# First head pair of the attention stage: keys and queries turned into two PSUM tiles, its four loads on SP's queue, the first batch's global keys and queries on ACT's queue

## Chip, cores and metric

The kernel runs on one core of a Trainium2 chip. The metric is the device time of one execution in microseconds (us), as the median of several runs. Engines are named as the profile names them: PE is TensorE, DVE VectorE, ACT ScalarE, POOL GpSimd and SP SyncE. SP and ACT both issue DMAs; "SPq" and "ACTq" are rows in which one of them does so.

## What is computed

An attention over local and global tokens (4 batches, 8 heads, 512 local and 32 global tokens, heads of 64), and behind it two gated feed-forward layers over the 2176 tokens that come out, of width 512.

```python
def _attn_ref(q_l, k_l, v_l, q_g, k_g, v_g):
    k_all = np.concatenate([k_g, k_l], axis=2)
    v_all = np.concatenate([v_g, v_l], axis=2)
    out_g = np.matmul(sm(scale * np.matmul(q_g, k_all.transpose(0, 1, 3, 2))), v_all)
    s_ll = np.where(mask, scale * np.matmul(q_l, k_l.transpose(0, 1, 3, 2)), -1e9)   # |i - j| <= 32
    s_lg = scale * np.matmul(q_l, k_g.transpose(0, 1, 3, 2))
    out_l = np.matmul(sm(np.concatenate([s_lg, s_ll], axis=-1)), np.concatenate([v_g, v_l], axis=2))
    return np.concatenate([out_g, out_l], axis=2)
...
x = attention, tokens by 512
x = (silu(x @ w_gate) * (x @ w_val)) @ w_out
h = x @ w_in
out = (h * tanh(softplus(h))) @ w_out2
```

## The kernel before, in words

Everything is in float32. The attention goes by pairs of heads: 16 pairs, four in each batch. Its work is cut into named tasks (line 231), each on one engine, and a string written by hand (`ORDER`, lines 222 to 229, read by `in_order`, line 243) says in which order the tasks are emitted. Each letter stands for a kind of task, and the kind says the engine ("Ak+1" is the keys' copy on its second engine). Nothing is reordered behind that list, so each engine meets its instructions in the order of the list, DMA issues of SP and ACT among them. The feed-forward layers follow under a scheduler of their own (`run`, line 1302), which goes by costs written in the kernel and knows nothing of the attention's times. So the change leaves its order as it was. The weights of the first layer are loaded and converted between the attention's tasks.

The tasks of the first pairs that matter here, with n the pair, b the batch and g the half of a pair's tokens:

- qk(n), `load_qk`, lines 167 to 176: four DMAs of 128 KB, two for the keys (`ks`) and two for the queries (`qs`). All are issued by SP, but for the two of the queries of pair 0, which ACT issues.
- gk(b, 0) and gk(b, 1), `load_glob`, lines 160 to 165: two DMAs of 32 KB each for the global keys of a batch, then two for its global queries, all on SP, into the one buffer `gkq`.
- A(n), line 273, PE: 8 transposes of the keys and 8 of the queries (line 213) into one PSUM tile of two banks. There are two such tiles. Ak(n) (lines 282, 236 and 238) copies the turned keys to `kt`, Aq(n) the turned queries to `qT`. For pair 0, Ak is on ACT and Aq on DVE, and Aq comes after Ak.
- AG(b, 0), line 467, PE: the transpose of the global keys; AGk(b), on ACT for batch 0, copies them to `gkT`. AG(b, 1) is the transpose of the global queries, and AGe(b) on DVE (line 478) scales them into `qgbd`.
- S(n, g), lines 297 to 308, PE: the scores, which need Aq(n), Ak(n) and AGk(b). M(n, g, i) on DVE (line 318) adds the mask and takes the smallest, E(n, g, i) on ACT (line 325) is the exponential.

The list begins: qk(0), A(0), Ak(0), Aq(0), gk(0, 0), AG(0, 0), AGk(0), S(0, 0), three M, E(0, 0, 0), M, qk(1), gk(0, 1), vg(0), qk(2), A(1), AG(0, 1), qk(3), Ak(1), AGe(0), S(0, 1), Aq(1), M, S(1, 0), GA(0), and so on. PE thus has, in this order: A(0), AG(0, 0), S(0, 0), A(1), AG(0, 1), S(0, 1), S(1, 0), GA(0).

Behind some PE tasks stand matmuls of zeros whose result nobody uses (`keep_busy`, line 150): 14 instructions at the start, and so many behind each PE task as the string `steady` (line 539) says: 6 instructions behind AG(0, 0), 2 behind AG(0, 1).

Of the kernel before, what the change touches and what calls it, by code (L numbers as in the profile page):

```python
# [21 lines left out]
def tile_attn_moe_moe2(  # L22
# [15 lines left out]
    nc = tc.nc  # L38
    B, H, SL, D = q_l.shape
# [5 lines left out]
    S = SG + SL  # L45
# [50 lines left out]
    vg = e_p.tile([128, 4, HP, D], F32, name="vg")  # L96
    vgb = e_p.tile([128, H, D], F32, name="vgb")
# [41 lines left out]
    def both(task):  # L139
        return PAIR[place[task]]  # L140
# [4 lines left out]
    QS, KS, VW, GK = {}, {}, {}, {}  # L145
# [4 lines left out]
    def keep_busy(bank, k):  # L150
        for i in range(k):
            nc.tensor.matmul(ONE[bank][:, 0:128], lhsT=zeros, rhs=zeros, start=True, stop=True)
# [7 lines left out]
    def load_glob(b, i):  # L160
        if i == 0:
            GK[b] = g_p.tile([128, 2, 128], F32, tag="gkq", name="gkq")
        for h in range(2):
            nc.sync.dma_start(out=GK[b][:, i, 64 * h:64 * h + 64],
                              in_=(k_g, q_g)[i][b].rearrange("(g h) p d -> h g p d", h=2)[h])

    def load_qk(b, hp):
        hs = slice(2 * hp, 2 * hp + 2)
        qs = qk_p.tile([128, 4, 2, D], F32, tag="qs", name="qs")
        ks = qk_p.tile([128, 4, 2, D], F32, tag="ks", name="ks")  # L170
        eng = nc.sync if b or hp else nc.scalar
        for h in range(2):
            nc.sync.dma_start(out=ks[:, :, h], in_=k_l[b, 2 * hp + h].rearrange("(c p) d -> p c d", p=128))
        for h in range(2):
            eng.dma_start(out=qs[:, :, h], in_=q_l[b, 2 * hp + h].rearrange("(c p) d -> p c d", p=128))
        QS[b, hp], KS[b, hp] = qs, ks

    def load_vg(b):
# [29 lines left out]
    def half(j):  # L208
        return slice(64 * j, 64 * j + 64)

    def transpose_half(out, src, j):

        nc.tensor.transpose(out, src, ident[half(j), half(j)])  # L213
# [2 lines left out]

    tasks = {}
    LETTERS = ascii_letters + digits + "!#$%&()*+-./:;<=>?@[]^_{|}~"
    KINDS = ("qk A Ak+1 Aq+1 gk AG AGk+1 S M E vg AGe Aq GA GG v R GGe w N GM C V+1 vgb GE GR GN D Cq Ak "
             "GT AGk Cf GV V GO Ch Xh Cl Xl Xh+1 GGe+1 GXh GXl F_g Ch+1 Cl+1 Ft F_v Fg Fp GXh+1 Fh Fl "  # L220
             "Fh+1 F2 Fy+1 Fy N+1").split()
    ORDER = "abcdefghiiijiaekabfaclhmihniiiijojphjjjjjiiiqbirjjsettucmveiiiwvwphxjjyzhjjjjABiijqiiiiiibjjjCjfttDEfFmv"
    ORDER += "nGHGvIGjhuIhiiiiJyjjjGqaabpKitBclidtLjjjiipMvvwsjINhzhjijjjiijAajBqtiiiiitLEHNOovPbNIJcCdvnjIheaGGGhiiiB"
    ORDER += "isjQjjjjqRiiibkQLtSppciumtbNyxvGSfwTUjcmjjjvCjjjVzhaAwWiiiihEsGeWiqRBaiXiiYGjjHjjjjGttvvnIGIjjuqythhJpKi"
    ORDER += "iiZiBsjjjpMiiii0btCRvaDSmLgvfSGGGGTIIjjjlhMzhiiiiij1jjjWqttAVbiWXiajLDBjjjmiNYN2vjjvInoqttIOhPE1iBjHuCii"
    ORDER += "jivkOvJGjINhGpSjIyspijiiixNbbjcGWacSjmdzGQjAqVhtthWiiiijeeijjjjERXBYHiiiCvvGaInGGGIhujjjhBiLqityKJiiijLt"
    ORDER += "bNiiiScMmNfvvFKISMzwZfbRjjjAhappaDjmj3ijjjiiiEl4hqstoniBHriiutivvww3yjLjj5jjjjhhiBiiziNiiiJiqjkLbbttjjjj"
    ORDER += "D3pANjjDZmd35jvqv2IntR1Ih4hpxtBiiiiijjVjEWHuXiiijjjjvvWjwwhyqYthiiijj0Jt1BpiiiZiziLjNApjvvjjjj33Rw5w34EL"
    ORDER += "Hq6B65vvw3IBLL5NNJNQRs"

    def task(name, engine, needs, work, banks=0, until=None):
        tasks[name] = engine, [x for x in needs if x is not None], work, banks, until
# [10 lines left out]
    def in_order():  # L243

        left, done = {}, []
        for n in tasks:
            left.setdefault(f"F_{n[3]}" if n[0] == "F" else n[0], []).append(n)
        free = {2: list(range(len(PAIR))), 1: list(range(len(ONE)))}
        until = {}
        for letter in ORDER:  # L250
            kind, _, other = KINDS[LETTERS.index(letter)].partition("+")
            n = left[kind].pop(0)
            engines, needs, _, banks, last = tasks[n]
            ON[n] = engines.split()[int(other or 0)]
            if not all(x in place for x in needs):
                raise RuntimeError(f"{n} comes before what it needs")
            place[n] = free[banks].pop(0) if banks else None
            if banks:
                until[last] = banks, place[n]
            if n in until:  # L260
                free[until[n][0]].append(until[n][1])
            SPARE_BANK[n] = free[1][0] if free[1] else None
            done.append(n)
        return done

    def add_pair(n):
        b, hp = divmod(n, HP)
        ago = lambda name, k: (name, n - k) if n >= k else None
        agog = lambda name, k, g: (name, n - k, g) if n >= k else None
        lastu = lambda name, m: (name, m // 2) if m >= 0 else None  # L270
        R = {}

        def qk():
            p = both(("A", n))
            for i, src in enumerate((KS[b, hp], QS[b, hp])):
                for r in range(4):
                    for j in range(2):
                        transpose_half(p[:, j, 256 * i + 64 * r:256 * i + 64 * r + 64],
                                       src[half(j), r].rearrange("p h d -> p (h d)"), j)
            R["pk"], R["pq"] = (p[:, :, 256 * i:256 * i + 256].rearrange("c j (r t) -> c r j t", t=64) for i in range(2))  # L280

        def keys():
            duplicate(("Ak", n), KT[n % 2][:, SG:SG + SL].rearrange("c (r j t) -> c r j t", j=2, t=64), R["pk"])
# [1 line left out]
        def queries():  # L285
            R["qT"] = qk_p.tile([128, 4, 128], F32, tag="qT", name="qT")
            dst = R["qT"].rearrange("c r (j t) -> c r j t", j=2)
            duplicate(("Aq", n), dst, R["pq"])

        task(("A", n), "PE", [("qk", n)], qk, 2, ("Aq", n))  # L290
        task(("Ak", n), "DVE ACT", [("A", n), lastu("GA", n - 2), agog("S", 2, 1)], keys)
        task(("Aq", n), "ACT DVE",
             [("A", n), ("Ak", n), agog("S", 2, 1)], queries)

# [85 lines left out]
        task(("Xl", n), "DVE", [("Xh", n)], lambda: x_parts(*args(), "l", ("Xl", n)))  # L382

        task(("qk", n), "SP", [ago("A", 2)], lambda: load_qk(b, hp))
        task(("v", n), "SP", [ago("D", 2), lastu("GO", n - 2)], lambda: load_v(b, hp))
        if hp % 2:
# [74 lines left out]
    def add_batch(b):  # L461
# [36 lines left out]
        for i in range(2):  # L498
            task(("gk", b, i), "SP", prev(("AG", b - 1, 1)), lambda i=i: load_glob(b, i))
# [3 lines left out]
    def add_convert(i):  # L503

        gen = None

        def go():
            nonlocal gen
            gen = gen or w_convert(converts.pop(0))
            next(gen, 0)  # L510

        task(("Cq", i), "ACT", [("w", i)] + ([("Cf", i - 1, 0)] if i else []), go)
        for j, room in enumerate((0.70, 1.20, 0.75, 0.80)):
            need = [("Cf", i, j - 1)] if j else [("Cq", i)] + ([("Cf", i - 1, 3), ("Cl", i - 2)][:i] if i else [])
            task(("Cf", i, j), "DVE", need, go)
        task(("Ch", i), "ACT DVE", [("Cf", i, 3)], go)
        task(("Cl", i), "POOL DVE", [("Ch", i)], go)
# [8 lines left out]
    def attention():  # L526


        for b in range(B):
            add_batch(b)  # L530
        for n in range(B * HP):
            add_pair(n)
        for i in range(8):
            task(("w", i), "SP", [("Cf", i - 2, 3)] if i > 1 else [], load_next)
        for i in range(6):
            add_convert(i)
        for i in FILL:
            add_fill(i)
        steady = iter("03001000014100000001")
        for name in in_order():  # L540
            tasks[name][2]()
            if tasks[name][0] == "PE" and SPARE_BANK[name] is not None:
                keep_busy(SPARE_BANK[name], int(next(steady, 0)))
# [165 lines left out]
    with tc.manual_schedule():  # L709
        setup()  # L710
        attention()
# [28 lines left out]
    def slots(p, shape, dtype, names):  # L740
        return [lambda name=name: p().tile(shape, dtype, tag=name, name=name) for name in names]
# [20 lines left out]
    GR = Ring(slots(lambda: s_p, [128, 512], F32, [f"s{i}" for i in range(5)]))  # L762
# [52 lines left out]
    for i in range(6):  # L815
        p = order[i]
# [603 lines left out]
```

## Time and profile before

| | |
|---|---|
| median of 3 runs | 880.22 us (879.88 to 880.99) |
| profiled execution, device time | 879.67 us |
| its span, first to last instruction | 877.9 us |
| mean granted TensorE clock | 0.999 |
| PE busy | 869.5 us, 99% of the span |
| DVE, POOL, ACT busy | 657.3, 519.0, 475.1 us |
| HBM traffic over the span | 176 GB/s |

The rows read for the prediction are all from the one profiled execution, and their times count from the start of its span. A row of the timeline has the start, the duration (of several instructions merged, where it ends with x2 or more, from the start of the first to the end of the last), the engine, the line of the kernel, the operation, the tile that is written and what is read; in brackets, how long the engine had been idle before and what released it.

### The profile page before, as it was taken

To read this page: it belongs to the slowest core of one execution; us is meant where nothing else is said; L and a number is where in the kernel's file an instruction comes from. 1 tells how busy PE (TensorE), PEld (TensorE's weight loads), DVE (VectorE), ACT (ScalarE), POOL (GpSimd) and SP (SyncE) were. 2 spreads that over 40 slices of the span, in tenths; PEclk is the share of its full clock that TensorE was granted. 3 is DMA by queue.
4 is the path that set the end of the run, shared out by engine and by line. 5 is a ranking of instruction groups with operands and counts; after the bars stand their busy time and mean duration, and the time that the engine had idled before them with its cause. 6 is when DMAs were issued, how large, how long until landed. Compare 5 with 4: busy or idle time off the path is not lost.

```text
span 877.9 us, 18526 instructions
## 1 busy us (share of the span) xinstructions
PE 869.5 (99%) x7004; PEld 805.9 (92%) x7004; DVE 657.3 (75%) x1243; ACT 475.1 (54%) x1153; POOL 519.0 (59%) x503
## 2 busy tenths in 40 slices
PE   8999999999999999999999999999999999999998
PEld 7788889989999999999999999898989898989896
DVE  5877777998988878778888899678886767543434
ACT  6888774544345554555555678754545454434341
POOL 4455645999985565566675799455466444433231
PEclk9999999999999999999999999999999999999999
DMA  7986743435556556557546436574747473535173
GB/s 177 207 188 135 169 98 74 161 104 195 182 178 244 174 180 224 173 156 246 174 157 226 157 140 255 171 251 156 264 143 253 164 256 116 184 108 193 58 255 143
DMA packets 157401, 155.61 MB, mean 177 GB/s; under 512 B 78976, under 2 KB 137856, under 8 KB 157312
## 3 DMA queue, kind: packets, MB, share of 16 engines
q1 hardware_dynamic: 155824, 153.38, 55.9%
q8 instruction: 55, 0.90, 0.4%
q10 hardware_dynamic: 1488, 1.05, 0.4%
q14 instruction: 34, 0.28, 0.1%
HBM read 132.12 MB, written 22.28 MB: 176 GB/s over the span
## 4 chain that ended last, share of the span: by engine, by line
PE 98%; DMA 1%; DVE 0%; ACT 0%; issue 0%; SPq 0%
PE p L1106 38%; PE p L1211 21%; PE p L997 15%; PE p L1063 9%; PE one L639 4%; PE pair L213 3%; PE pair L304 2%; PE one L371 2%; PE one L375 2%; PE one L445 1%; PE one L399 1%; PE pair L307 1%; DMA gkq<-in_q_g 1%; DMA ks<-in_k_l 0%; ACT kt L236 0%
## 5 line engine op out<-in xcount | busy, mean ns | idle before, releaser
L1106 PE MATMUL p<-xh,w 128*128 128x384 f32 (+1 forms) x992 | 257.4, 326 | 0.0
L1211 PE MATMUL p<-w,a 128*128 128x512 f32 x816 | 194.3, 391 | 0.0
L1211 PEld LDWEIGHTS p<-w,a 128*128 128x128 f32 x816 | 152.2, 188 | 29.9
L1106 PEld LDWEIGHTS p<-xh,w 128*128 128x128 f32 x992 | 176.8, 188 | 1.4
L1106 PE MATMUL p<-xl,w 128*128 128x384 f32 (+1 forms) x496 | 161.5, 326 | 0.0
L1118 ACT ACTIVATE b<-p 128x384 f32<-128x384 f32 (+1 forms) x144 | 68.1, 473 | 160.6 <-PE p L1106 156.5
L997 PE MATMUL p<-a,w 128*128 128x384 f32 (+2 forms) x768 | 142.8, 334 | 0.0
L997 PEld LDWEIGHTS p<-a,w 128*128 128x128 f32 x768 | 130.6, 188 | 2.8
L1221 DVE TENSOR_TENSOR y<-p,y 128x512 f32<-128x512 f32 x119 | 82.1, 690 | 66.1 <-PE p L1211 64.8
L1027 POOL TENSOR_TENSOR a<-b,a 128x384 fp32r<-128x384 f32 (+1 forms) x57 | 60.4, 1060 | 110.3 <-ACT a L1025 76.7
L810 DVE TENSOR_TENSOR b<-p,b 128x384 f32<-128x384 f32 (+1 forms) x144 | 76.6, 532 | 63.3 <-PE p L1106 48.1
L857 POOL TENSOR_TENSOR w<-cx,w 128x256 fp32r<-128x256 f32 (+1 forms) x94 | 101.5, 1092 | 35.4 <-ACT w L856 30.0
L1106 PE MATMUL p<-e,w 128*128 128x384 f32 (+1 forms) x528 | 100.8, 328 | 0.0
L1027 POOL TENSOR_TENSOR a<-s,a 128x384 fp32r<-128x384 f32 (+2 forms) x54 | 63.9, 1185 | 55.7 <-ACT a L1025 55.5
L1106 PEld LDWEIGHTS p<-xl,w 128*128 128x128 f32 x496 | 93.1, 188 | 1.4
L1106 PEld LDWEIGHTS p<-e,w 128*128 128x128 f32 x528 | 90.0, 188 | 1.1
L1006 DVE TENSOR_TENSOR y<-p,y 128x384 f32<-128x384 f32 (+2 forms) x116 | 62.7, 543 | 19.7 <-PE p L997 18.5
L1063 PE MATMUL p<-xh,w 128*128 128x384 f32 (+1 forms) x256 | 72.7, 356 | 0.0
L580 DVE SCALAR_TENSOR_TENSOR fl<-q,st 128x512 f32<-128x512 f32 x68 | 62.0, 912 | 5.0 <-ACT q L572 4.8
L1025 ACT ACTIVATE a<-s 128x384 fp32r<-128x384 f32 (+2 forms) x88 | 45.2, 515 | 37.7 <-DVE s L1049 36.7
L584 DVE SCALAR_TENSOR_TENSOR cx<-fl,cx 128x512 uint32<-128x512 uint32 x68 | 63.5, 934 | 1.1
L586 DVE SCALAR_TENSOR_TENSOR cx<-st,cx 128x512 uint32<-128x512 uint32 x68 | 63.3, 932 | 0.7
(151 smaller groups left out, 1486.6 us busy)
## 6 DMA issues: line engine op xcount, KB each, us to landing
e<-td SPq DMA_DIRECT2D x76, 384.0 KB, 4.2
xh<-td SPq DMA_DIRECT2D x38, 384.0 KB, 3.3
xl<-td SPq DMA_DIRECT2D x38, 384.0 KB, 4.1
st<-in_moe_w_out SPq DMA_DIRECT2D x28, 512.0 KB, 3.7
st<-in_moe_w_in SPq DMA_DIRECT2D x16, 512.0 KB, 4.1
vw<-in_v_l SPq DMA_DIRECT2D x14, 512.0 KB, 6.2
e<-td SPq DMA_DIRECT2D x22, 320.0 KB, 5.6
st<-in_moe_w_gate SPq DMA_DIRECT2D x12, 512.0 KB, 4.7
```

The source lines that it names most:

```text
L584: nc.vector.scalar_tensor_tensor(x, fu, 0xC0000000, x, op0=ALU.bitwise_and, op1=ALU.bitwise_or)
L586: nc.vector.scalar_tensor_tensor(x, STG.pop(p)[:, :, 0], 29, x, op0=ALU.logical_shift_right, op1=ALU.bitwise_or)
L810: return lambda e: vec(e).tensor_tensor(out=out(), in0=a(), in1=b(), op=op)
L857: add(lo or [("POOL", PO(n))], 0, lambda e: vec(e).tensor_tensor(out=dst(1), in0=src(), in1=dst(0).bitcast(F32), op=ALU.subtract), r=[rd, ...
L997: nc.tensor.matmul(ps.h[:, 0:n], lhsT=a.h[:, d], rhs=b.h[:, at:at + n], start=(i == 0 and j == 0), stop=(i == len(ws) - 1 and j == 2))
L1006: add("DVE", DV(n), lambda e: nc.vector.tensor_tensor(out=ya, in0=ps.h[:, 0:n], in1=ya, op=ALU.add), r=[ps], w=yt)
L1027: t.append(add(either(n), 0, lambda e: vec(e).tensor_tensor(out=dst(1), in0=get(), in1=dst(0).bitcast(F32), op=ALU.subtract), r=[v, (av[0] ...
L1063: nc.tensor.matmul(ps.h[:, 0:n], lhsT=a.h[:, d], rhs=b[:, c, c0:c0 + n], start=(c == 0 and j == 0), stop=(c == KD - 1 and j == 2))
L1106: nc.tensor.matmul(ps.h[:, 0:n], lhsT=w.h[:, 256 * a + 128 * c:256 * a + 128 * c + 128], rhs=xs[b][:, c, :], start=(start and c == 0 and j ...
L1118: add("ACT", AC(n), lambda e: nc.scalar.activation(out=dst.h[:, 0:n], in_=src.h[:, 0:n], func=AF.Copy), r=[sv], w=[dst])
L1211: nc.tensor.matmul(ps.h, lhsT=a.h[:, d], rhs=b.h, start=(i == 0 and q == 0), stop=(i == len(ws) - 1 and q == 2))
L1221: add("DVE", DV(512), lambda e: nc.vector.tensor_tensor(out=ya, in0=pa(), in1=ya, op=ALU.add), r=[ps], w=tok)
```

## The change

The two DMAs of pair 0's queries go to SP's queue, behind those of its keys. The four DMAs of batch 0's global keys and queries go to ACT's queue. The turning of pair 0 becomes two tasks, A(0) for the keys and a new At(0) for the queries, each with a PSUM tile of its own; Ak(0) waits for A(0) alone and Aq(0) for At(0) alone. In the list of the order one task is added, At(0) right behind A(0); every other task keeps its place (the string differs in nearly all its letters because the new kind shifts the alphabet by one). So gk(0, 0) stands behind Ak(0) as before, and gk(0, 1) behind E(0, 0, 0). `steady` gets a zero in front, so that the zero matmuls stay where they were.

```diff
 def load_glob(b, i):
...
         for h in range(2):
-            nc.sync.dma_start(out=GK[b][:, i, 64 * h:64 * h + 64],
-                              in_=(k_g, q_g)[i][b].rearrange("(g h) p d -> h g p d", h=2)[h])
+            (nc.sync if b else nc.scalar).dma_start(out=GK[b][:, i, 64 * h:64 * h + 64],
+                                                    in_=(k_g, q_g)[i][b].rearrange("(g h) p d -> h g p d", h=2)[h])
 def load_qk(b, hp):
...
-        eng = nc.sync if b or hp else nc.scalar
...
-            eng.dma_start(out=qs[:, :, h], in_=q_l[b, 2 * hp + h].rearrange("(c p) d -> p c d", p=128))
+            nc.sync.dma_start(out=qs[:, :, h], in_=q_l[b, 2 * hp + h].rearrange("(c p) d -> p c d", p=128))
...
+        def turn_qk(p, i):
+            src = (KS, QS)[i][b, hp]
+            for r in range(4):
+                for j in range(2):
+                    transpose_half(p[:, j, 256 * i + 64 * r:256 * i + 64 * r + 64],
+                                   src[half(j), r].rearrange("p h d -> p (h d)"), j)
+            R["pq" if i else "pk"] = p[:, :, 256 * i:256 * i + 256].rearrange("c j (r t) -> c r j t", t=64)
+
         def qk():
-            p = both(("A", n))
-            for i, src in enumerate((KS[b, hp], QS[b, hp])):
-                for r in range(4):
-                    for j in range(2):
-                        transpose_half(p[:, j, 256 * i + 64 * r:256 * i + 64 * r + 64],
-                                       src[half(j), r].rearrange("p h d -> p (h d)"), j)
-            R["pk"], R["pq"] = (p[:, :, 256 * i:256 * i + 256].rearrange("c j (r t) -> c r j t", t=64) for i in range(2))
+            turn_qk(both(("A", n)), 0)
+            if n:
+                turn_qk(both(("A", n)), 1)
...
-        task(("A", n), "PE", [("qk", n)], qk, 2, ("Aq", n))
+        task(("A", n), "PE", [("qk", n)], qk, 2, ("Aq", n) if n else ("Ak", n))
+        if not n:
+            task(("At", n), "PE", [("qk", n)], lambda: turn_qk(both(("At", n)), 1), 2, ("Aq", n))
         task(("Ak", n), "DVE ACT", [("A", n), lastu("GA", n - 2), agog("S", 2, 1)], keys)
         task(("Aq", n), "ACT DVE",
-             [("A", n), ("Ak", n), agog("S", 2, 1)], queries)
+             [("A", n), ("Ak", n), agog("S", 2, 1)] if n else [("At", n)], queries)
...
-        steady = iter("03001000014100000001")
+        steady = iter("003001000014100000001")
```

## Rows read from the trace of the kernel before

**Rows 1.** The page: busy time of each engine, and the chain by engine.

```profile
PE 869.5 (99%) x7004; PEld 805.9 (92%) x7004; DVE 657.3 (75%) x1243; ACT 475.1 (54%) x1153; POOL 519.0 (59%) x503
...
PE 98%; DMA 1%; DVE 0%; ACT 0%; issue 0%; SPq 0%
```

**Rows 2.** Waits of PE, 0 to 110 us, then 24 us to the end: total, times, longest.

```profile
PE one L467 <- DMA gkq<-in_q_g: 1.1, 1, 1.1
...
PE pair L304 <- DVE pt L238: 0.4, 1, 0.4
```

**Rows 3.** Windows view: stretch, length, then busy PE, PEld, DVE, ACT, POOL, clock, DMA.

```profile
9.60:12.00 2.40, 2.39 (x68) 1.89 (x70) 1.90 (x13) 2.40 (x11) 0.00 (x0) 1.00 0.92 209
12.00:16.00 4.00, 3.73 (x68) 2.96 (x64) 2.87 (x20) 3.21 (x13) 2.19 (x3) 1.00 0.88 196
16.00:20.00 4.00, 3.83 (x101) 3.45 (x103) 3.04 (x13) 4.00 (x20) 1.80 (x3) 1.00 0.89 220
20.00:22.50 2.50, 2.50 (x65) 2.17 (x61) 1.81 (x11) 1.98 (x9) 2.50 (x4) 1.00 0.94 210
```

**Rows 4.** Timeline: DMA issues of SP and ACT, and ACT's first instruction.

```profile
0.79 1.11 ACTq L175 DMA_DIRECT2D qs<-in_q_l  x2
1.83 1.34 SPq L164 DMA_DIRECT2D gkq<-in_k_g  x2
1.92 1.28 ACT L236 ACT_TABLE_LOAD   x1 [1.92 <-issue]
5.39 1.15 SPq L164 DMA_DIRECT2D gkq<-in_q_g  x2
10.72 1.81 SPq L173 DMA_DIRECT2D ks<-in_k_l  x2
18.05 1.11 SPq L164 DMA_DIRECT2D gkq<-in_q_g  x2
```

**Rows 5.** Timeline: PE, ACT and DVE from the first transposes to S(0, 1).

```profile
4.99 0.69 PE L213 MATMUL pair<-ident,ks 64*128 64x64 f32 x8 [0.53 <-DMA ks<-in_k_l]
5.44 0.49 PE L213 MATMUL pair<-ident,qs 64*128 64x64 f32 x8
5.87 0.32 PE L467 MATMUL one<-ident,gkq 128*128 128x128 f32 x1
5.96 0.60 ACT L236 ACTIVATE kt<-pair 128x512 f32<-128x512 f32 x1 [2.76 <-PE pair L213]
6.03 0.83 PE L152 MATMUL one<-zeros 128*128 128x128 f32 x6
6.46 0.27 ACT L236 ACTIVATE gkT<-one 128x128 f32<-128x128 f32 x1
6.59 0.69 DVE L238 COPY qT<-pair 128x512 f32<-128x512 f32 x1 [3.66 <-ACT kt L236]
7.43 0.45 PE L304 MATMUL pair<-kt,qT 64*64 64x128 f32 x8 [0.57 <-DVE qT L238]
8.85 0.43 ACT L325 ACTIVATE sm<-sm,nb 128x160 f32<-128x160 f32 x1 [2.12 <-DVE nb L318]
8.88 0.33 PE L467 MATMUL one<-ident,gkq 128*128 128x128 f32 x1
9.18 0.19 ACT L325 ACTIVATION_READ_ACCUMULATOR sm<-sm,nb 128x1 f32 x1
9.60 0.45 PE L304 MATMUL pair<-kt,qT 64*64 64x128 f32 x8 [0.17 <-DVE nb L318]
```

**Rows 6.** DMA view, 0 to 130 us: KB each, median us from issue to landing.

```profile
vg<-in_v_g SPq DMA_DIRECT2D x16, 32.0 KB, 2.4
...
qs<-in_q_l ACTq DMA_DIRECT2D x2, 128.0 KB, 3.4
```

**Rows 7.** Chain of waits, 0 to 25 us: start, duration, what.

```profile
18.63 4.87 DMA gkq<-in_q_g
```

**Rows 8.** Instruction groups of PE, 0 to 4.6 us, then 5.8 to 17 us.

```profile
L152 PE MATMUL one<-zeros 128*128 128x128 f32 x14 | 3.4, 432 | 1.1 <-DVE zeros L148 1.1
...
L152 PE MATMUL one<-zeros 128*128 128x128 f32 x20 | 3.4, 290 | 0.0
```

More of the change, by code (lines that the diff above doesn't have):

```diff
@@ L218, in tile_attn_moe_moe2 @@
     LETTERS = ascii_letters + digits + "!#$%&()*+-./:;<=>?@[]^_{|}~"
-    KINDS = ("qk A Ak+1 Aq+1 gk AG AGk+1 S M E vg AGe Aq GA GG v R GGe w N GM C V+1 vgb GE GR GN D Cq Ak "
-             "GT AGk Cf GV V GO Ch Xh Cl Xl Xh+1 GGe+1 GXh GXl F_g Ch+1 Cl+1 Ft F_v Fg Fp GXh+1 Fh Fl "
+    KINDS = ("qk A At Ak+1 Aq+1 gk AG AGk+1 S M E vg AGe Aq GA GG v R GGe w N GM C V+1 vgb GE GR GN D Cq "
+             "Ak GT AGk Cf GV V GO Ch Xh Cl Xl Xh+1 GGe+1 GXh GXl F_g Ch+1 Cl+1 Ft F_v Fg Fp GXh+1 Fh Fl "
              "Fh+1 F2 Fy+1 Fy N+1").split()
[L222 to L229, printed above, removed]
+    ORDER = "abcdefghijjjkjaflabgadminjiojjjjkpkqikkkkkjjjrbjskktfuuvdnwfjjjxwxqiykkzAikkkkBCjjkrjjjjjjbkkkDkguuEFgGn"
+    ORDER += "woHIHwJHkivJijjjjKzkkkHraabqLjuCdmjeuMkkkjjqNwwxtkJOiAikjkkkjjkBakCrujjjjjuMFIOPpwQbOJKdDewokJifaHHHijjj"
+    ORDER += "CjtkRkkkkrSjjjblRMuTqqdjvnubOzywHTgxUVkdnkkkwDkkkWAiaBxXjjjjiFtHfXjrSCajYjjZHkkIkkkkHuuwwoJHJkkvrzuiiKqL"
+    ORDER += "jjj0jCtkkkqNjjjj1buDSwaETnMhwgTHHHHUJJkkkmiNAijjjjjk2kkkXruuBWbjXYjakMECkkknjOZO3wkkwJopruuJPiQF2jCkIvDj"
+    ORDER += "jkjwlPwKHkJOiHqTkJztqjkjjjyObbkdHXadTkneAHRkBrWiuuiXjjjjkffjkkkkFSYCZIjjjDwwHaJoHHHJivkkkiCjMrjuzLKjjjkM"
+    ORDER += "ubOjjjTdNnOgwwGLJTNAx0gbSkkkBiaqqaEknk4jkkkjjjFm5irtupojCIsjjvujwwxx4zkMkk6kkkkiijCjjAjOjjjKjrklMbbuukkk"
+    ORDER += "kE4qBOkkE0ne46kwrw3JouS2Ji5iqyuCjjjjjkkWkFXIvYjjjkkkkwwXkxxizrZuijjjkk1Ku2Cqjjj0jAjMkOBqkwwkkkk44Sx6x45F"
+    ORDER += "MIr7C76wwx4JCMM6OOKORSt"
     def task(name, engine, needs, work, banks=0, until=None):
```

## The prediction, made before the changed kernel ran

> **What bounds the kernel now.** I read the page first. PE is busy 99% of the span, and the chain that ended last is 98% PE [rows 1]. So over the long run time is won or lost only where PE stands still or does more work. The second view is therefore PE's waits. Up to 110 us there are few, and the longest that bears on this change is 1.1 us for the global queries of batch 1, at the transpose of line 467; behind 24 us only one of 0.4 us is left up to the end [rows 2]. So whatever PE is late by 24 us, it is late at the end too, less 0.4 us at most. The change lies ahead of that point, and the question is when PE gets through the first 24 us. Third, the windows of that stretch: from S(0, 1) at 9.60 us to 22.5 us PE is busy in all but 0.45 us (0.01, 0.27, 0.17 and 0 in the four stretches) [rows 3]. Its order is fixed, so a late S(0, 1) moves this whole stretch, and at most 0.45 us of the delay is absorbed inside it.
>
> Fourth, the timeline of the issues. ACT issues the two query loads at 0.79 us for 1.11 us, to 1.90, and its table load starts at 1.92 [rows 4]. ACT does one thing after the other: an instruction behind a DMA issue waits for it, and I take it that a DMA issue behind an instruction that waits is held up as well. SP issues its loads likewise in the order of the list.
>
> **The change part by part.** *The place of the global loads decides.* On SP, gk(0, 0) had only DMA issues ahead of it and went out at 1.83 us, gk(0, 1) at 5.39 [rows 4]. On ACT the list puts gk(0, 0) behind Ak(0), a copy that waits for PE, and gk(0, 1) behind E(0, 0, 0), which waits for the scores. PE's own order then is A(0), At(0), AG(0, 0), S(0, 0), A(1), AG(0, 1), S(0, 1): two of these transposes each wait for a load that ACT can issue only late. Step by step:
>
> 1. Keys turned. The 8 transposes of the keys start at 4.99 us, when their load is there, and last 0.69 us, to 5.68. Ak(0) started at 5.96 behind all 16; alone it starts at 5.70 and ends at 6.30 (0.60 us) [rows 5].
> 2. Global keys issued. No row of before shows an issue behind a copy. The lower end is the time when ACT's wait is released, 5.70 (the issue runs beside the copy), the upper the copy's end, 6.30. I take the middle, 6.0. Two issues take 1.11 us on ACT [rows 4], so the second starts at 6.56.
> 3. Landing. A load of the same size on SP takes 2.4 us from issue, the only ones on ACT's queue, of four times the size, 3.4 [rows 6]; the slowest of this very kind, 4.87 [rows 7]. I take 2.9, midway between the two nearest: 9.46. AG(0, 0) starts at 9.5 instead of 5.87 [rows 5].
> 4. S(0, 0). Behind AG(0, 0) stand 6 zero matmuls, which end 0.99 us after its start (5.87 to 6.86); the copy to `gkT` fits beside them (0.32 and 0.27 us) [rows 5]. So S(0, 0) starts at 10.5 instead of 7.43, 3.1 us late.
> 5. Global queries issued. From S(0, 0) to the start of E(0, 0, 0) it is 1.42 us, to its end 1.94 (7.43 to 8.85 and to 9.37) [rows 5]. So the issue starts between 11.9 and 12.45; I take 12.2, and 12.75 for the second.
> 6. Landing, in a stretch where the DMA engines are 0.88 to 0.92 busy [rows 3]: here I take ACT's 3.4 us [rows 6], which gives 16.15. AG(0, 1) starts at 16.2 instead of 8.88, S(0, 1) 0.55 us later (0.72 before, of which 0.17 was a wait for a minimum that now is long done) [rows 5]: 16.75 instead of 9.60, **7.15 us late**.
>
> What is given back: PE's 1.1 us wait for batch 1's global queries [rows 2] goes, since PE comes there some 7 us later. Those loads need the one `gkq` buffer, free when AG(0, 1) is done at 16.5. SP wins 1.4 us at the start (1.34 and 1.15 us of issues go [rows 4], 1.11 comes, by ACT's row), but its key loads at 10.72 [rows 4] then wait for A(1), which follows S(0, 0) and has turned the keys of pair 1 by about 11.9: 1.2 us late. The queries of batch 1 then land at 18.63 + 1.2 + 4.87 = 24.7 us [rows 7], and PE wants them at about 29. So 4 us of cover remain. Of the 0.45 us of small gaps I take 0.2. Last, the keys of pair 0 no longer share the DMA engines with their queries; PE's zero matmuls end at 4.5 us (1.1 + 3.4) [rows 8], so step 1 can gain between 0 and 0.5; I take 0.25.
>
> Costed at nothing: the turning in two tiles (the same 16 transposes and two copies; Aq(0) is ready about 3 us before AGk(0) allows S(0, 0); without that cover its path would be a gain, see the first rival); the late issue of pair 0's queries (they go behind the keys at 1.83 us and have till about 9 before anything needs them); ACT's 1.11 us of second issues, ahead of Ak(1), Aq(1) and three exponentials, which all fit before S(0, 1).
>
> **Sum:** 7.15 - 1.1 - 0.2 - 0.25 = 5.6 us. The profiled execution took 879.67 us (span 877.9), which gives 885.3; the median of the runs lies 0.55 us above it, so 885.8 us. A measurement of this kernel can tell about 0.2%, or 1.8 us, from no change.
>
> **The rivals.** *Not slower: the loads are not held up.* Should ACT issue the global loads at 0.79 us, as it did the queries [rows 4], none of steps 2 to 6 holds. Then Ak(0) starts at 5.70, Aq(0) when At(0) ends (5.93, to 6.62 with 0.69 us [rows 5]), and S(0, 0) when the zero matmuls end, 6.86, 0.6 us earlier; SP is 1.4 us ahead and PE's wait at line 467 shrinks. The gain is 0.6 to 1.4 us, or 879.2 with 1.0: inside the 0.2%. The point at which it decides: the global keys must be there by 5.9 us, so issued by about 3 us. For it speaks that the queue itself is free; against it the list and the row of the table load [rows 4]. The Trainium skill ("DMA: Bandwidth & Descriptors", section "Issuing engines are not separate DMA queues") says that DMAs of different engines share the same 16 DMA engines, and that issuing from several saves only the issuing time. By that rule alone this rival's gain is all that the move can bring; what an issue waits for on ACT it leaves open.
>
> *Slower still: PE at a lower clock.* The zero matmuls took 432 ns each in the first 4.6 us and 290 later [rows 8], which fits the lower of PE's two levels (1.2 and 2.4 GHz) after no activity; the granted clock of the stretches shown reads 1.00 throughout [rows 3]. After the change PE stands still from about 6.2 to 9.5 us and from 12.1 to 16.2. If it falls back there, the price is at most what the start shows, 14 times 142 ns = 2.0 us, for the second gap: 887.8 us. Against it: no row of before has PE slow after a gap, and none has such a gap. The Trainium skill ("TensorE: Matmul & The Clock Gate", Part 1) says that the throttled state is the default and activity lifts it; the start agrees, the rest no run here shows.
>
> **How the numbers follow.** The forecast has 0.60, the lower clock 0.25, the loads that are not held up 0.12; 0.03 is left for what I don't see. Bounds of the forecast: the landings 2.4 to 4.87 us (-0.5 to +2.0 for the keys, -1.0 to +1.5 for the queries), the issues 0.3 us each way twice, the start 0.25, the gaps 0.2. All at the good end give about 3.0 us, 882.7; all at the bad end 10, which is far less likely than one landing there, 887.8, with half of the clock's price 889. The range goes from 882.6 to 889.5; it leaves out the first rival, 0.12. Chances: slower 0.86, within 0.2% 0.12, faster 0.02.
>
> **What would show it.** In the changed profile: ACT's issues of `gkq` at about 6 and 12 us; PE waiting for DMA of `gkq` from about 6 to 9.5 and from 12 to 16 us; S(0, 1) at 16 to 17.5; no wait for `gkq` at batch 1; and all later PE work shifted by 5 to 6 us. I am wrong if ACT's issues stand near 0.8 us, if PE passes AG(0, 1) before 12 us, or if a shift at 20 us is no longer there at 100.

## The result, and the profile after

The changed kernel takes **888.35 us** (median of 5 runs, 887.19 to 889.25) against 879.88 for the kernel before beside it: a ratio of 1.0090, with a 95% interval of 1.0077 to 1.0104. That is 8.5 us slower. The forecast was slower by 5.6 us, 885.8, with a range of 882.6 to 889.5. The direction, the place and the two waits held; the size was too small by about a third. The profiled execution took 889.25 us, with a span of 887.5 (877.9 before), so it is 9.6 us that its trace has to explain.

First PE's waits, from 0 to 120 us, with the total, the number and the longest:

```profile
PE one L472 <- DMA gkq<-in_q_g: 4.1, 1, 4.1
PE one L472 <- DMA gkq<-in_k_g: 3.3, 1, 3.3
...
PE pair L309 <- DVE pt L237: 0.6, 1, 0.6
```

Line 472 is the transpose that was line 467. The wait of 1.1 us for batch 1 [rows 2] is gone, and two longer ones stand at batch 0's loads. Behind 30 us only 0.9 us of waits are left, so what is lost is lost early. The timeline of the changed kernel shows how (columns as in [rows 4, 5]):

```profile
0.79 1.28 ACT L235 ACT_TABLE_LOAD   x1 [0.79 <-PEq L1412]
4.39 0.69 PE L212 MATMUL pair<-ident,ks 64*128 64x64 f32 x8
5.13 0.60 ACT L235 ACTIVATE kt<-pair 128x512 f32<-128x512 f32 x1 [3.06 <-PE pair L212]
5.13 1.74 ACTq L164 DMA_DIRECT2D gkq<-in_k_g  x2
9.13 0.45 PE L472 MATMUL one<-ident,gkq 128*128 128x128 f32 x1 [3.33 <-DMA gkq<-in_k_g]
9.37 1.49 PE L152 MATMUL one<-zeros 128*128 128x128 f32 x6
10.79 0.71 PE L309 MATMUL pair<-kt,qT 64*64 64x128 f32 x8
12.22 0.52 PE L212 MATMUL pair<-ident,ks 64*128 64x64 f32 x8
12.88 0.43 ACT L330 ACTIVATE sm<-sm,nb 128x160 f32<-128x160 f32 x1 [2.99 <-DVE nb L323]
12.88 0.57 ACTq L164 DMA_DIRECT2D gkq<-in_q_g  x1
13.50 0.57 ACTq L164 DMA_DIRECT2D gkq<-in_q_g  x1
17.10 0.45 PE L472 MATMUL one<-ident,gkq 128*128 128x128 f32 x1 [4.10 <-DMA gkq<-in_q_g]
17.90 0.70 PE L309 MATMUL pair<-kt,qT 64*64 64x128 f32 x8
22.80 0.45 PE L309 MATMUL pair<-kt,qT 64*64 64x128 f32 x8
26.06 0.47 PE L212 MATMUL pair<-ident,sm 64*128 64x64 f32 x8 [0.24 <-ACT qT L235]
29.20 1.09 PE L376 MATMUL one<-pt,vg 128*64 128x128 f32 x16
32.51 0.33 PE L472 MATMUL one<-ident,gkq 128*128 128x128 f32 x1
33.38 0.46 PE L212 MATMUL pair<-ident,sm 64*128 64x64 f32 x8 [0.32 <-ACT qT L235]
```

ACT issues the global keys at the moment when its copy Ak(0) is released, and the global queries when the first exponential is. Both loads then take their time to land, and PE stands still. The chain of waits of the same execution gives the landings behind the second issue of each:

```profile
6.32 2.67 DMA gkq<-in_k_g
...
13.50 3.46 DMA gkq<-in_q_g
```

To follow the delay past 10 us, five more lines of the timeline of the kernel before are needed:

```profile
12.50 0.45 PE L304 MATMUL pair<-kt,qT 64*64 64x128 f32 x8
16.05 0.46 PE L213 MATMUL pair<-ident,sm 64*128 64x64 f32 x8 [0.23 <-ACT qT L236]
19.18 1.09 PE L371 MATMUL one<-pt,vg 128*64 128x128 f32 x16
23.63 0.30 PE L467 MATMUL one<-ident,gkq 128*128 128x128 f32 x1 [1.07 <-DMA gkq<-in_q_g]
24.09 0.46 PE L213 MATMUL pair<-ident,sm 64*128 64x64 f32 x8
```

In the table, C(n, g) are the transposes of a pair's weights behind the exponentials and D(n) the products with its values; all times are starts in us.

| PE's work | before | after | late by |
|---|---|---|---|
| A(0), keys turned | 4.99 | 4.39 | -0.60 |
| AG(0, 0) | 5.87 | 9.13 | 3.26 |
| S(0, 0) | 7.43 | 10.79 | 3.36 |
| AG(0, 1) | 8.88 | 17.10 | 8.22 |
| S(0, 1) | 9.60 | 17.90 | 8.30 |
| S(1, 1) | 12.50 | 22.80 | 10.30 |
| C(0, 0) | 16.05 | 26.06 | 10.01 |
| D(0) | 19.18 | 29.20 | 10.02 |
| AG(1, 1) | 23.63 | 32.51 | 8.88 |
| C(1, 0) | 24.09 | 33.38 | 9.29 |
| end of the span | 877.9 | 887.5 | 9.6 |

The two big jumps are the two waits; the second, 4.86 us, is larger than its wait of 4.10, since PE also took longer from S(0, 0) on. A third, 2.0 us between S(0, 1) and S(1, 1), has no wait at all: the same matmuls took 4.90 us instead of 2.90. The windows view says why (stretch, length, busy PE, PEld, DVE, ACT, POOL, then the granted clock and the DMA engines' share):

```profile
9.60:12.00 2.40, 2.40 (x37) 2.17 (x37) 0.00 (x0) 0.28 (x1) 0.00 (x0) 0.50 0.48 109
16.00:18.00 2.00, 0.90 (x7) 0.71 (x11) 0.34 (x2) 0.41 (x3) 0.00 (x0) 0.50 1.19 242
18.00:20.00 2.00, 2.00 (x52) 2.00 (x56) 0.76 (x6) 0.16 (x1) 0.00 (x0) 0.50 0.96 192
20.00:22.00 2.00, 2.00 (x24) 1.08 (x21) 1.68 (x15) 2.00 (x11) 0.00 (x0) 0.50 0.62 196
22.80:24.00 1.20, 1.20 (x38) 1.06 (x34) 0.26 (x3) 0.00 (x0) 1.20 (x3) 1.00 1.31 263
```

Behind both gaps PE's granted clock is 0.50, the lower of its two levels (1.2 of 2.4 GHz), where the kernel before had 1.00 [rows 3]. The one transpose of line 472 shows it too: 0.45 us in both places, 0.33 again at 32.51. Just ahead of the second gap PE had been fast (8 transposes in 0.52 us at 12.22, against 0.69 at 4.39), so there it fell.

### The profile page after: what moved, and what is told of

It is laid out like the page before. It is cut to its first block, busy times and chain, and to the rows that moved or that the text cites. A ratio compares the mean times of both kernels' runs of the same rounds, so it can differ in the third digit from the quotient of the medians.

```text
span 887.5 us, 18526 instructions
## 1 busy us (share of the span) xinstructions
PE 873.4 (98%) x7004; PEld 809.0 (91%) x7004; DVE 657.8 (74%) x1243; ACT 475.7 (54%) x1153; POOL 518.4 (58%) x503
## 4 chain that ended last, share of the span: by engine, by line
PE 98%; DMA 1%; issue 0%; DVE 0%; ACT 0%; ACTq 0%; DVEq 0%
PE p L1111 37%; PE p L1216 21%; PE p L1002 15%; PE p L1068 8%; PE one L644 4%; PE pair L212 3%; PE pair L309 2%; PE one L376 2%; PE one L380 2%; PE one L450 1%; PE one L404 1%; PE pair L312 1%; PE one L152 1%; DMA gkq<-in_q_g 0%; DMA gkq<-in_k_g 0%
## 5 line engine op out<-in xcount | busy, mean ns | idle before, releaser
L342 POOL TENSOR_TENSOR sm<-sm,rc 128x512 f32<-128x512 f32 x30 | 31.2, 1040 | 56.5 <-DVE rc L336 38.5
```

## The experiments

**The place of the loads, undone and moved.** The first run puts the four loads back on SP.

```diff
-            (nc.sync if b else nc.scalar).dma_start(out=GK[b][:, i, 64 * h:64 * h + 64],
+            nc.sync.dma_start(out=GK[b][:, i, 64 * h:64 * h + 64],
```

> The changed kernel with the four global loads back on SP's queue; the queries of pair 0 on SP and the two PSUM tiles stay. If the place of the global loads behind ACT's copy and exponential is the whole cause, this is the kernel before again: 879 to 881 us, AG(0, 1) near 9 to 10 us. If the split in two tiles or the queries' move costs something by itself, it stays above 882 us.

Measured: 880.78 us against 879.97, ratio 1.0011 (1.0002 to 1.0020). Nine tenths of the loss are gone, and the rest is smaller than 0.2%. PE passes both transposes early (timeline):

```profile
6.70 0.30 PE L472 MATMUL one<-ident,gkq 128*128 128x128 f32 x1 [0.67 <-DMA gkq<-in_k_g]
...
9.69 0.30 PE L472 MATMUL one<-ident,gkq 128*128 128x128 f32 x1 [0.37 <-DMA gkq<-in_q_g]
```

The second leaves the loads on ACT but puts them at the head of the list, right behind qk(0), which SP issues (in the letters of the changed kernel, f is gk).

```diff
-    ORDER = "abcdefghijjjkjaflabgad...
+    ORDER = "affbcdeghijjjkjalabgad...
```

> The changed kernel with the global loads on ACT's queue, but put first in the list, ahead of the copy Ak(0), so that ACT issues all four from 0.8 us on. If being held up behind instructions that wait is the cause, the loss is gone: 878.3 to 880 us, all four issued by 3.1 us. If ACT's queue serves such small loads late by itself, PE still waits at AG(0, 0) or AG(0, 1) and the time is above 883 us.

Measured: 880.64 us, ratio 1.0008 (0.9999 to 1.0017). The loss is gone, so it was not ACT's queue in itself that made it, but what stands ahead on it. But 0.6 us over the upper end expected shows a new wait: with the global loads on ACT, pair 0's queries on SP come late, and PE waits 1.67 us for them. Its timeline:

```profile
0.79 1.73 ACTq L164 DMA_DIRECT2D gkq<-in_k_g  x2
2.55 1.10 ACTq L164 DMA_DIRECT2D gkq<-in_q_g  x2
...
6.75 0.69 PE L212 MATMUL pair<-ident,qs 64*128 64x64 f32 x8 [1.67 <-DMA qs<-in_q_l]
7.38 0.47 PE L472 MATMUL one<-ident,gkq 128*128 128x128 f32 x1
```

Behind that wait the transpose takes 0.47 us, as at the lower clock, and S(0, 1) starts at 12.38 us, 2.8 late. This execution (881.33 us) is 1.4 us slower than the median of the kernel before, so about half of this lateness is made up again.

The third makes that one edit in the kernel before: the global loads on ACT at their place in the list, with nothing else changed.

```diff
-            nc.sync.dma_start(out=GK[b][:, i, 64 * h:64 * h + 64],
+            (nc.sync if b else nc.scalar).dma_start(out=GK[b][:, i, 64 * h:64 * h + 64],
```

> The kernel before with one edit alone: the global loads of batch 0 on ACT's queue, at their place in the list. Theory: the whole loss and a little more, since the copy Ak(0) starts at 5.96 us here instead of 5.13: 888 to 890 us, PE waiting 3 to 4 us twice. If the loss needs the split or the queries on SP as well, it is under 885 us.

Measured: 890.37 us, ratio 1.0114 (1.0100 to 1.0128). The edit alone makes the whole loss, and 1 to 2 us more, a little over the range expected; the copy that holds it up starts at 6.13 us here, 1.0 later than in the changed kernel. PE's waits in this run:

```profile
PE one L467 <- DMA gkq<-in_k_g: 4.7, 1, 4.7
PE one L467 <- DMA gkq<-in_q_g: 3.9, 1, 3.9
```

**The lower clock apart from the waits.** Zero matmuls in PE's gaps leave the loads where they are and keep PE at work while it would wait.

```diff
-        steady = iter("003001000014100000001")
+        steady = iter([0, 10, 3, 0, 12, 1] + [int(c) for c in "000014100000001"])
```

> The changed kernel with zero matmuls put into PE's two gaps: 10 (20 instructions, about 2.8 us) behind At(0), 12 (24 instructions, about 3.3 us) behind A(1). The waits stay, the gaps go. Theory: of the 8.5 us about 2.7 are PE at the lower clock after the gaps (0.7 behind the first, 2.0 behind the second), so 885.1 to 886.3 us with the granted clock at 1.00 throughout. If the two waits make up all of it, the time stays at 888 us; if the zeros run past the landings it rises.

Measured: 885.71 us, ratio 1.0065 (1.0052 to 1.0077), where the changed kernel had 1.0090: 2.6 us by the medians, where 2.7 had been expected. The windows read 1.00 in both stretches, and the transposes are back at 0.30 us:

```profile
9.60:12.00 2.40, 2.40 (x58) 2.17 (x57) 0.71 (x5) 0.62 (x3) 0.00 (x0) 1.00 0.63 142
...
16.00:20.00 4.00, 4.00 (x120) 3.19 (x114) 3.33 (x23) 2.58 (x12) 0.69 (x1) 1.00 0.87 210
```

For a comparison on one chip the changed kernel ran again, beside a version with zeros in the second gap alone (`[0, 0, 3, 0, 12, 1]` in the line above).

> The changed kernel once more, on the same chip as the next run: 887.2 to 889.3 us as before.

> The changed kernel with 12 zero matmuls (24 instructions) behind A(1) alone: the second gap is filled, the first is not. Theory: the lower clock behind the second gap costs about 2.0 us and that goes, the 0.7 us behind the first stays: 886 to 887 us, against the changed kernel in the run beside it. If PE's clock in the second stretch does not hang on that gap, it stays at 888 us or rises.

Measured: 889.22 us (888.73 to 889.38) for the first, ratio 1.0096 (1.0076 to 1.0115); 885.77 (885.42 to 886.93) for the second, 1.0062 (1.0043 to 1.0082). So 3.4 us go, more than the 2.0 expected. The timeline of the second splits them:

```profile
5.70 0.47 PE L212 MATMUL pair<-ident,qs 64*128 64x64 f32 x8 [0.62 <-DMA qs<-in_q_l]
9.15 0.45 PE L472 MATMUL one<-ident,gkq 128*128 128x128 f32 x1 [2.99 <-DMA gkq<-in_k_g]
...
13.48 0.54 ACTq L164 DMA_DIRECT2D gkq<-in_q_g  x1
15.92 0.30 PE L472 MATMUL one<-ident,gkq 128*128 128x128 f32 x1
16.37 0.45 PE L309 MATMUL pair<-kt,qT 64*64 64x128 f32 x8
...
19.06 0.45 PE L309 MATMUL pair<-kt,qT 64*64 64x128 f32 x8
```

From AG(0, 1) to S(1, 1) it is 3.14 us, against 5.70 in the changed kernel (17.10 to 22.80): 2.6 us of clock. Most of that lies between S(0, 1) and S(1, 1), where nothing waits for a load: 2.69 us here, 4.90 there. The rest is the landing: the queries were there within 2.4 us of their second issue, against 3.46. From 13.5 to 15.8 us the DMA engines moved 89 GB/s here and 186 there, and SP's key loads took longer to go out in this execution (2.29 us against 0.92). Whether the zeros have a part in that stays open. The first gap, left open here, shows PE falling as well: its transposes were fast ahead of it (8 in 0.47 us) and slow behind it (0.45 us for one).

Set against the kernel before beside them, both gaps filled (885.71 us against 879.97) and the second alone (885.77 against 880.40) come to the same. So these medians don't show what the first gap's lower clock costs. In the traces the version with both filled is 0.7 us ahead at S(1, 1) (18.34 against 19.06): it saves 1.4 us of clock behind the first gap, but its loads land later (3.15 and 2.81 us behind the second issues, against 2.69 and at most 2.35).

**Each wait alone.** First the global queries right behind the global keys, so that only the copy holds them up:

```diff
-    ORDER = "abcdefghijjjkjaflabgad...
+    ORDER = "abcdeffghijjjkjalabgad...
```

> The changed kernel with the global queries put right behind the global keys in the list: all four loads on ACT behind the copy Ak(0), none behind the exponential. Theory: the two waits add up one behind the other, so one of them goes. PE still waits about 3.3 us at AG(0, 0), but the queries land by about 11 us and AG(0, 1) at 13 us does not wait: 3.3 us late, less the 1.1 us wait at batch 1, plus 0.7 to 2 us of the lower clock behind the first gap, 882.5 to 884.5 us. If the first wait alone made the loss, the time stays above 886 us.

Measured: 883.25 us, ratio 1.0041 (1.0029 to 1.0054), within the range expected. PE waits at AG(0, 0) and not at AG(0, 1):

```profile
9.22 0.45 PE L472 MATMUL one<-ident,gkq 128*128 128x128 f32 x1 [2.93 <-DMA gkq<-in_k_g]
...
13.10 0.33 PE L472 MATMUL one<-ident,gkq 128*128 128x128 f32 x1
```

Then the keys back on SP and the queries alone behind the exponential:

```diff
-            (nc.sync if b else nc.scalar).dma_start(out=GK[b][:, i, 64 * h:64 * h + 64],
+            (nc.sync if b or i == 0 else nc.scalar).dma_start(out=GK[b][:, i, 64 * h:64 * h + 64],
```

> The changed kernel with the global keys back on SP; the global queries stay on ACT behind E(0, 0, 0). The second wait alone. E(0, 0, 0) can start near 9 us, so the queries land near 13 us and AG(0, 1) is some 3.4 us later than with both loads on SP (9.7 us there); less the wait at batch 1, plus up to 2 us of the lower clock behind the gap: 882.8 to 885.5 us. If a load behind the exponential alone cost nothing, 881 us.

Measured: 886.79 us against 880.40, ratio 1.0067 (1.0049 to 1.0085), over the expected range. The trace shows a step that I had not counted. PE ran at its lower clock already from AG(0, 0) on, after a wait of only 0.69 us:

```profile
6.70 0.45 PE L472 MATMUL one<-ident,gkq 128*128 128x128 f32 x1 [0.69 <-DMA gkq<-in_k_g]
...
10.46 1.14 ACTq L164 DMA_DIRECT2D gkq<-in_q_g  x1
...
15.54 0.45 PE L472 MATMUL one<-ident,gkq 128*128 128x128 f32 x1 [4.98 <-DMA gkq<-in_q_g]
```

So the exponential and the issue behind it came 1.5 us later than I had worked out, the first issue took 1.14 us, and the wait grew to 5.0 us. The run with all four loads on SP stood still just as long (0.67 us) and ran at the higher clock behind it (0.30 us for the same transpose). In both, the 8 transposes of the keys ahead of the wait took 0.69 us, as at the lower clock. Whether PE fell behind the short wait or had not yet risen stays open.

**The other parts, and a better version.** The split in two tiles alone, in the kernel before (both DMA edits undone):

> The kernel before with the two PSUM tiles and the task At(0) alone; all loads on their queues of before. Theory: Ak(0) starts 0.3 us earlier and Aq(0) no longer waits for it, so S(0, 0) can start up to 0.5 us earlier, of which the zero matmuls ahead of it let little through: 879.4 to 880.3 us, no change that can be told. If the split costs something by itself, 881 us or more.

Measured: 880.03 us against 879.71, ratio 1.0009 (1.0000 to 1.0018). Ak(0) starts at 5.72 instead of 5.96 and S(0, 0) at 7.03 instead of 7.43, but at AG(0, 1) PE then waits 0.34 us for the global queries, and passes it at 8.94 against 8.88: the 0.4 us are given back at the next load. So the split costs nothing that can be told, and brings nothing. Then all of the first loads but pair 0's keys on ACT, the global ones ahead of the copy, without and with the split:

> The kernel before (one tile, pair 0's queries on ACT) with the global loads of batch 0 on ACT too, put ahead of the copy in the list. If being held up was the only harm in ACT's queue, no loss is left, and SP, 2.5 us of issues lighter, may win up to 1 us: 879 to 880.2 us. If loads on two queues slow each other so that PE waits for the first keys or queries, as it did 1.7 us when the queries were behind the keys on SP, it is 881 us or more.

> The split in two tiles with pair 0's queries and all global loads of batch 0 on ACT, the global loads put first in the list. Theory: as the kernel before or a little faster, 878.8 to 880.2 us. A loss of over 1 us would say that the split or ACT's queue costs something in itself.

Measured: 881.53 us (1.0021, 1.0012 to 1.0030) and 881.60 (1.0019, 1.0011 to 1.0028): about 1.8 us slower, both over what I expected. In the version without the split, first two lines of the timeline, then one of the chain of waits:

```profile
5.69 1.28 ACT L236 ACT_TABLE_LOAD   x1 [5.69 <-DMA qs<-in_q_l]
...
7.46 0.30 PE L467 MATMUL one<-ident,gkq 128*128 128x128 f32 x1 [1.69 <-DMA gkq<-in_k_g]
```

```profile
3.08 4.24 DMA gkq<-in_k_g
```

Six issues hold ACT's own table load till 5.69 us, and the copy with it till 6.98. But it is the load that PE waits for: the global keys land 4.24 us behind their second issue, and PE can turn them only at 7.46 us, against 5.87 with SP's issues [rows 5]; with the split it is 7.46 as well. The two profiled executions (880.63 and 879.61 us) are the fastest of their versions, so they don't show all of the 1.8 us. Last, only the global queries on ACT, ahead of the copy, in the kernel before:

> The kernel before with the global keys on SP at their old time, ahead of all but the first two loads, and only the global queries on ACT, right behind pair 0's queries and ahead of the copy. ACT is then free for its table load at about 3.5 us, in time for the copy at 6. Theory: 879 to 880.2 us, as the kernel before or up to 1 us faster, since SP has two issues less. If any extra load at the start makes PE wait for the first loads, 881 us or more.

Measured: 880.03 us against 880.40, ratio 0.9995 (0.9982 to 1.0007). It is as good as the kernel before and not better. No version that ran beats it.

## Why the prediction came out as it did

*The place of the loads decides* (steps 2 to 6): right. The run with that edit alone makes the whole loss, and the run without it is back within 0.2%.

*Step 1, keys turned:* the keys were turned at 4.39 us, 0.6 earlier than before, right behind the zero matmuls; I had taken 0.25 of a possible 0.5.

*Step 2, issue beside the copy or behind it:* beside it, the lower end (both rows start at 5.13 us). But the first issue took until 6.28, 1.15 us, where I had 0.56 from ACT's other loads, so the second started at 6.32. That this is my 6.56 less the 0.25 of step 1 is luck: an issue that came early and one that took long cancel.

*Steps 3 and 6, the landings:* 2.67 and 3.46 us, against 2.9 and 3.4. Near, but 2.67 to 3.15 and 2.4 to 3.46 us in the versions with and without zeros show how far they move.

*Steps 4 to 6, what PE does behind each load:* **here the sum failed.** From AG(0, 0) to S(0, 0) I had 0.99 us; it took 1.66. From S(0, 0) to the exponential I had 1.42; it took 2.09. From AG(0, 1) to S(0, 1) I had 0.55; it took 0.80. All these spans were taken from [rows 5], where PE was not behind a long gap, and here PE ran at 0.50 of its clock. Without these 1.6 us S(0, 1) would have come at about 16.3 us, 6.7 late, near the 6.9 of the forecast (7.15 less 0.25); it came 8.30 us late.

*What is given back:* right in each part. The wait at batch 1 went (10.02 us late at D(0), 8.88 at AG(1, 1): 1.14); the small gaps gave 0.29. But 0.4 us came back behind it at C(1, 0), where PE now waits 0.32 us for ACT's copy (9.29 late).

**The missing term is the lower clock.** The sum put it at nothing. I had it as a rival with a chance of 0.25 and a price of "at most" 2.0 us for the second gap, and none for the first. The table shows 2.0 between S(0, 1) and S(1, 1) alone; with the 0.25 ahead of that and 1.3 us behind the first gap it is 3.6 us in this execution. 5.6 + 3.6 and the 0.4 at C(1, 0) give 9.6, what the profiled execution lost; the smaller misses cancel. The second trace of the changed kernel (889.38 us) has the same spans: 1.66, 2.10, 0.81 and, between S(0, 1) and S(1, 1), 4.98 us. Both are among its slowest executions (887.19 to 889.38), so what the clock costs at the median stays open; there the loss is 8.5 us, and the runs with zeros take back 2.6 and 3.4 of it. That the gaps are the cause is shown by the stretch from S(0, 1) to S(1, 1): 2.69 us where zeros filled the gap ahead of it, 4.90 where nothing did. What failed is the weighing: I counted against the rival that no row of before has PE slow behind a gap, though no such gap was there to see, and the zeros at the start [rows 8] were the one row that bore on it. The Trainium skill ("TensorE: Matmul & The Clock Gate", Part 1), which has the throttled state as the default, agrees with these traces: 0.50 behind both gaps, 1.00 where zeros filled them.

The range held, but two of the signs that I had named did not: S(0, 1) came at 17.90 us, not between 16 and 17.5, and the later work was shifted by 9.6 us in the profiled execution, not by 5 to 6. The range was wide enough through its bounds for the landings and half of the clock's price, 889. Its lower end, 882.7, was counted from the profiled 879.67 us while the forecast was counted from the median; on one footing it is 883.2.

*The first rival* (the loads are not held up) fell: ACT's issues stand at 5.13 and 12.88 us. What it would bring could be seen when the loads were put first: nothing, as pair 0's queries then land late. That fits the rule of the Trainium skill that I had named there ("DMA: Bandwidth & Descriptors", "Issuing engines are not separate DMA queues"): SP's issues were saved, and PE waited 1.67 us for its queries instead.

## What to carry to other kernels

A DMA issue is an instruction of the engine that makes it. Before a load is moved to a less busy engine, look at what stands ahead of it there and what that waits for; here a copy and an exponential, the latter itself fed by the first of the loads, turned issues at 1.8 and 5.4 us into issues at 5.1 and 12.9. And a wait of TensorE can have two prices: the gap, and the slower matmuls behind it. The second was paid behind the two gaps here wherever zeros did not fill them, and not behind the 1.07 us of batch 1 in the kernel before (0.30 us for the transpose). Rows with PE busy throughout tell nothing of it, so it belongs in the sum as soon as a new gap is forecast.

## What the runs showed of the hardware

- PE ran at its lower clock behind gaps of 3.3 and 4.1 us (granted clock 0.50), and in the second case it was back only between 22 and 22.8 us. In two executions it ran slowly behind a wait of only 0.5 to 0.7 us near the start, in a third with the same wait it did not. These are three versions, with one trace of each; what decides it stays open.
- The granted clock of the windows doesn't always show it. In the run with the one edit in the kernel before, all stretches read 1.00, and the transposes behind its two gaps took 0.45 us, as those at 0.50 did (a line of the windows and one of the timeline below). So it is behind the first gap in the second trace of the changed kernel. The duration of one and the same small matmul was the better witness.

```profile
9.60:12.00 2.40, 1.21 (x6) 1.24 (x7) 0.00 (x0) 0.28 (x1) 0.00 (x0) 1.00 0.56 127
...
10.79 0.45 PE L467 MATMUL one<-ident,gkq 128*128 128x128 f32 x1 [4.70 <-DMA gkq<-in_k_g]
```

- On ACT a DMA issue runs beside the copy that was released at the same moment. The first global load that ACT issued took 1.12 to 1.34 us in the runs, the others about 0.55. That is not the copy's 0.60 and an issue behind it: with the loads put first, no copy ahead, the first took 1.15 too.
